# A pair's V products one step later, z's low products last, and GpSimd in program order in the first unit

## The chip, the core and the metric

One core of one Trainium2 chip. The metric is the device time of one execution in microseconds. The kernel before was timed in three runs; its profile comes from one more execution.

## What is computed

Attention with a window and a few global keys, then two feed-forward stages. The reference, cut:

```python
scores = scale * np.matmul(q, k.transpose(0, 1, 3, 2)) + bias     # q, k, v: 4 x 8 heads x 768 x 64
a = np.exp(where(keep, scores, -1e9) - max); a = a / (a.sum(-1) + 1e-9)
x = np.matmul(a, v)                                               # rows become 3072 x 512
h = x @ w_in                                                      # 512 -> 2048
z = (h * np.cos(h)) @ w_out                                       # 2048 -> 512
# then: rows with z @ w_skip > 0 go to the best of 8 experts by z @ w_gate:
y = z + gate * (np.maximum(z @ w1[e], 0) @ w2[e])                 # the other rows keep z
```

## The kernel before

The 3072 rows are worked in eight units of 384 tokens (`UT`), half a batch each. `unit(u)` runs 16 steps f, one for each block of 128 columns of w_in, and each step has two slots, 2f and 2f + 1. A step does: the h products of block f (`moe_h`, 12 matmuls of 384 columns, line 526; the weights and x are each split into a high and a low part, so three products stand for one); what is entered for the even slot; the angle, the sine and the product h cos h (`moe_g`); the split of later weight blocks (`split_hi`, `split_lo`, whose low part wi_lo is VectorE's line 492); the z products of block f - 2 (`moe_z`, line 565, nine matmuls of 512 columns into three PSUM banks, one for each tile of 128 tokens); and what is entered for the odd slot. `h cos h` is split by `split_g` into ghi (ScalarE, line 536) and glo (GpSimd, line 537). In the first unit `split_g` of a block is put off to the next step (`late_split`), behind that step's h products.

While unit u - 1 runs, the attention of unit u is worked in between, in four pairs p of heads, eight slots apart. The table `ev` (and `late`, run after `ev` and the rest of the slot) holds which part goes into which slot, counted from s0 = 32 (u - 1) + 8 p - 3: transposes of q and k (`att_Tq`, `att_Tk`) at s0 - 5 and s0 - 4; score products (`att_S`, line 396) of the three tiles at s0, s0 + 1, s0 + 2, each into two PSUM banks that VectorE empties while it adds the bias (line 401); the exponent on ScalarE, the sum's reciprocal on VectorE and the scaling of the six tiles sc on GpSimd (`att_E`, lines 415, 420, 425) late in s0 + 2; transposes of the probabilities (`att_P`, ps_p, lines 437 and 440) at s0 + 5 to s0 + 7; the products with v (`att_V`, ps_v, lines 452 and 457) at s0 + 9, which ScalarE empties into xhi (line 466) and VectorE into xlo (line 467). The rows of v before a tile are loaded into the one buffer ld_va by four DMAs on SP's queue (`att_load_va`) at s0 + 2. So the pair's values come two slots after the last ps_p, in the same slot as the second score products of the next pair, in front of them. From the second unit on, scores, transposes and values share a rotation of three PSUM banks (`ps_a`, tag "ps"). The values of the first pair go to slot 6 of a unit, of the second to slot 14, of the third to 22, of the last to 30.

The routing of a finished unit runs on VectorE in the next one: from slot 4 or 6 on, two products a slot, 27 in all (junk, line 623). Through units 1 to 6 a part of the weights is loaded again on SP's queue (ck) and checked on VectorE (cmin, line 298). In the first unit the weights are also converted, block by block (`conv_tick`: ScalarE line 212, VectorE lines 219 and 223, and in the next tick GpSimd line 230).

The order on an engine: inside `tc.manual_schedule(engines=...)` the engines named run in the order in which the program writes their work; the others are ordered by a planner that takes what it thinks is ready, the earlier in the program first. TensorE is in written order throughout, ScalarE in the units; VectorE, GpSimd and SP's queue are left to the planner in units 0 to 6. The planner's order is fixed when the program is built.

Of the kernel before, what the change touches and what calls it, by code (L numbers as in the profile page):

```python
# [20 lines left out]
P = 128  # L21
# [16 lines left out]
def kernel(  # L38
# [7 lines left out]
    NP = H // 2  # L46
# [146 lines left out]
    wo_hi = wp.tile([P, FC, DM], F32R, name="wo_hi", tag="b1")  # L193
    wo_lo = wp.tile([P, FC, DM], F32R, name="wo_lo", tag="b2")
# [81 lines left out]
    def conv_to(m, f):  # L276
        while (m, min(f, FC - 1)) not in conv_done:
            conv_tick()
# [26 lines left out]
    att = {}  # L305
# [102 lines left out]
    def att_E(u, p):  # L408
        d = att[u, p]
        sm = d["sum"]  # L410
        for t in range(HT):
            c0 = 104 if u % 2 == 0 and t == 0 else 0
            s = d["s"][t]
            for j in range(2):
                nc.scalar.activation(  # L415
                    out=s[:, j, c0:NW], in_=s[:, j, c0:NW], func=AF.Exp,
                    scale=-1.0, bias=d["m"][:, t, j:j + 1], accum_out=sm[:, t, j:j + 1],
                )
        nc.vector.tensor_scalar(out=sm, in0=sm, scalar1=1e-9, scalar2=None, op0=ALU.add)
        nc.vector.reciprocal(sm, sm)  # L420
        for t in range(HT):
            c0 = 104 if u % 2 == 0 and t == 0 else 0
            s = d["s"][t]
            for j in range(2):
                nc.gpsimd.tensor_scalar(  # L425
                    out=s[:, j, c0:NW], in0=s[:, j, c0:NW],
                    scalar1=sm[:, t, j:j + 1], scalar2=1.0, op0=ALU.mult, op1=ALU.mult,
                )
# [46 lines left out]
    zt = {}  # L475
# [82 lines left out]
    def moe_z(u, f, tiles=range(HT)):  # L558
        if f == 0 and u not in zt:
            zt[u] = [ps_z.tile([P, DM], F32, name="zp") for _ in range(HT)]  # L560
        ghi, glo = gq[u, f]
        for t in tiles:
            sl = slice(t * P, (t + 1) * P)
            for n, (a, b) in enumerate(((ghi, wo_hi), (ghi, wo_lo), (glo, wo_hi))):
                nc.tensor.matmul(  # L565
                    zt[u][t], a[:, sl], b[:, f, :],
                    start=(f == 0 and n == 0), stop=(f == FC - 1 and n == 2),
                )

# [154 lines left out]
    def at(slot, fn, *a, tail=False):  # L724
        (late if tail else ev).setdefault(slot, []).append((fn, a))
# [6 lines left out]
    for u in range(1, NU):  # L732
        for p in range(NP):
            s0 = HS * (u - 1) + PS * p - 3
            at(s0 - 12, att_load, u, p)
            at(s0 - 5, att_load_v, u, p)
            at(s0 - 5, att_Tq, u, p)
            at(s0 - 4, att_Tk, u, p)
            for t in range(HT):
                at(s0 + t, att_S, u, p, t)  # L740
                at(s0 + 5 + t, att_P, u, p, t)
            at(s0 + 9, att_V, u, p)
            at(s0 + 2, att_load_va, u, p)
            at(s0 + 2, att_E, u, p, tail=True)
    for i in range(4 * FC):
        s0 = HS + 8 + i * (HS * (NU - 2) - 24) // (4 * FC)
        at(s0, check_load, i)
        at(s0 + 2, check_min, i)
# [29 lines left out]
    for p in range(NP + 1):  # L778
        if p < NP:
            if p > 1:  # L780
                att_load_v(0, p)
            for t in range(HT):
                att_S(0, p, t)
            if p + 1 < NP:
                att_Tq(0, p + 1)
                att_Tk(0, p + 1)
            if p + 1 < NP:
                fill(p + 1)
            if p + 2 < NP:
                att_load(0, p + 2)  # L790
            att_E(0, p)
        warm(2, ps_a, "ps")
        if p > 0:
            for t in range(HT):
                att_P(0, p - 1, t)
            att_V(0, p - 1)
            if p < NP:
                att_load_va(0, p)
        conv_tick()
# [8 lines left out]
    def early():  # L808
        for s_ in range(min(list(ev) + list(late)), 0):
            run_slot(ev, s_)  # L810
            run_slot(late, s_)
        for f in range(2):
            conv_to(0, f)
            split_hi(f)
        split_lo(0)

    def unit(u):
        for f in range(FC):
            s_ = HS * u + 2 * f
            moe_h(u, f)  # L820
            if late_split:
                split_g(*late_split.pop())
            run_slot(ev, s_)
            moe_g(u, f)
            run_slot(late, s_)
            if u == 0:
                conv_to(0, f + 2)
                if f >= LAG:
                    conv_to(1, f - LAG)

            split_hi((f + 2) % FC, act=u == 0)
            split_lo((f + 1) % FC)
            if u == 0:
                for _ in range(TICKS[f % len(TICKS)]):
                    conv_tick()

                for i in range(f * E * NB0 // FC, (f + 1) * E * NB0 // FC):
                    e, j = divmod(i, NB0)
                    nc.sync.dma_start(xs[e * CAP + j * P:e * CAP + (j + 1) * P, :], pad)
            zf = u * FC + f - LAG  # L840
            if zf >= 0:
                moe_z(zf // FC, zf % FC)
                if zf % FC == FC - 1:
                    done = zf // FC
                    routes[done] = Route(rp_["p"], HT, done * UT)
                    routes[done].evac(zt[done])
            run_slot(ev, s_ + 1)
            run_slot(late, s_ + 1)
# [121 lines left out]

    with tc.manual_schedule(engines={mybir.EngineType.PE}):
        early()
        with tc.manual_schedule(engines={mybir.EngineType.Activation}):
            unit(0)
            conv_to(1, FC - 1)
        route_setup()
# [3 lines left out]
        with tc.manual_schedule(engines={mybir.EngineType.SP}):  # L980
            with tc.manual_schedule(engines={mybir.EngineType.Activation}):


                u = NU - 1
# [6 lines left out]
                for f in range(FC + 1):  # L991
# [26 lines left out]
                    if f < LAG:  # L1018
                        moe_z(u - 1, FC - LAG + f)
                        if f == LAG - 1:  # L1020
                            routes[u - 1] = Route(rp_["p"], HT, (u - 1) * UT, zpool=rp_["z"])
                            routes[u - 1].evac(zt[u - 1])
# [37 lines left out]
                with tc.manual_schedule(engines={mybir.EngineType.Pool, mybir.EngineType.DVE}):  # L1060
# [51 lines left out]
                    for n in range(NS + LAG):  # L1112
                        e, f = divmod(n, F2C)
# [13 lines left out]
                        if n >= LAG:  # L1127
                            e, f = divmod(n - LAG, F2C)
# [312 lines left out]
```

## Time and profile before

| | us |
|---|---|
| median of 3 runs | 1008.06 (1006.95 to 1009.19) |
| the profiled execution | 1010.82 |
| its span, first to last instruction | 1009.1 |
| TensorE busy in the span | 953.4 (94%) |
| VectorE busy | 751.7 (74%) |
| ScalarE busy | 535.3 (53%) |
| GpSimd busy | 532.8 (53%) |

The span runs through a first attention pass without h and z (to about 50 us), the first unit (50 to 165 us), units 1 to 6 (to about 716 us), the last unit (to about 798 us) and the experts. Busy times of TensorE include the stretches in which its clock was granted at the lower level, so a busy TensorE is not always one at its peak. In a timeline, the number in brackets is how long the engine stood before the instruction, and what let it go on.

### The profile page before, as it was taken

What the parts mean: (1) busy time and instruction counts of PE and PEld (TensorE: products, weight loads), DVE (VectorE), ACT (ScalarE), POOL (GpSimd) and SP (SyncE); (2) the same over time, 40 slices, a digit from 0 to 9 for tenths busy, and PEclk for the clock granted to TensorE, in tenths of its full rate; (3) what the DMA queues carried; (4) which work ended last, traced back from release to release, by engine and by line L of the source; (5) the groups of instructions that cost most, each with busy time, mean ns of one, the idle gap of its engine ahead of it and who ended that gap; (6) DMA issues with size and microseconds to landing.
All of it is one profiled execution on the core that took longest, in us unless ns stands there. A gap on an engine that the chain in (4) does not pass through costs nothing.

```text
span 1009.1 us, 17130 instructions
## 1 busy us (share of the span) xinstructions
PE 953.4 (94%) x5677; PEld 803.4 (80%) x5677; DVE 751.7 (74%) x1871; ACT 535.3 (53%) x1295; POOL 532.8 (53%) x707
## 2 busy tenths in 40 slices
PE   8878899999999999999999999999999889999996
PEld 4566678878878888887888788878898779999995
DVE  6679987986796689569757955885572387888882
ACT  5768878557656665665666566656463121111110
POOL 3657765545464546545454545465462355555662
PEclk7899899999999999999999999999999999999998
DMA  7497865234433443431112112100104384666400
GB/s 188 100 231 204 244 168 184 70 91 118 129 84 99 115 120 81 121 94 31 30 43 72 29 29 51 54 15 11 39 13 182 134 319 185 209 231 227 176 19 22
DMA packets 144385, 115.08 MB, mean 114 GB/s; under 512 B 100247, under 2 KB 116631, under 8 KB 144160
## 3 DMA queue, kind: packets, MB, share of 16 engines
q1 hardware_dynamic: 141056, 107.89, 36.1%
q0 software_dynamic: 3200, 5.98, 1.6%
q8 instruction: 47, 0.77, 0.3%
q14 instruction: 50, 0.41, 0.1%
q10 hardware_dynamic: 32, 0.03, 0.0%
HBM read 97.36 MB, written 21.05 MB: 117 GB/s over the span
## 4 chain that ended last, share of the span: by engine, by line
PE 57%; DVE 26%; DMA 5%; issue 5%; ACT 4%; POOL 2%; SPq 0%; POOLq 0%; ACTq 0%; DVEq 0%
PE zp L565 14%; PE hp L526 14%; DVE junk L623 9%; PE hp L946 9%; PE zp L965 9%; DVE wi_lo L492 4%; PE ps_s L396 3%; DVE r L509 2%; DVE r L552 2%; DVE sc L401 2%; DMA ck<-in_moe_w_out_dram 1%; PE ps_p L437 1%; DVE w_in_sb L223 1%; PE ps_v L457 1%; DMA st<-in_moe_w_out_dram 1%
## 5 line engine op out<-in xcount | busy, mean ns | idle before, releaser
L537 POOL TENSOR_TENSOR glo<-r,ghi 128x384 fp32r<-128x384 f32 x115 | 133.1, 1157 | 180.0 <-ACT ghi L536 149.6
L526 PE MATMUL hp<-xhi,wi_hi 128*128 128x384 f32 x492 | 177.2, 360 | 2.1 <-DVE r L552 1.3
L526 PE MATMUL hp<-xhi,wi_lo 128*128 128x384 f32 x492 | 166.9, 339 | 0.9 <-DVE wi_lo L492 0.9
L526 PE MATMUL hp<-xlo,wi_hi 128*128 128x384 f32 x492 | 165.9, 337 | 0.0
L492 DVE TENSOR_TENSOR wi_lo<-w_in_sb,wi_hi 128x512 fp32r<-128x512 f32 x128 | 114.6, 896 | 51.6 <-PE hp L526 16.8
L623 DVE CUSTOM_DVE_ANT_0 junk<-r_zr,wrep 128x512 bf16<-128x512 f32 x162 | 140.8, 869 | 8.3 <-ACT r_zr L585 6.4
L565 PE MATMUL zp<-wo_hi,ghi 128*128 128x512 f32 x345 | 146.7, 425 | 0.0
L565 PE MATMUL zp<-wo_hi,glo 128*128 128x512 f32 x345 | 137.3, 398 | 8.3 <-POOL glo L537 8.2
L565 PE MATMUL zp<-wo_lo,ghi 128*128 128x512 f32 x345 | 136.1, 395 | 0.0
L425 POOL TENSOR_SCALAR sc<-sc,sm 128x232 f32<-128x232 f32 (+1 forms) x180 | 93.6, 541 | 61.5 <-DVE sm L420 42.3
L514 ACT ACTIVATE r<-r,halfpi 128x384 f32<-128x384 f32 x128 | 79.0, 617 | 82.1 <-DVE r L509 81.0
L536 ACT CAST ghi<-r 128x384 fp32r<-128x384 f32 x115 | 59.0, 513 | 115.4 <-DVE r L552 114.3
L526 PEld LDWEIGHTS hp<-xhi,wi_hi 128*128 128x128 f32 x492 | 93.2, 189 | 16.8 <-issue 9.3
L951 ACT ACTIVATE hh<-hp 128x256 fp32r<-128x256 f32 x64 | 24.7, 387 | 152.2 <-PE hp L946 152.2
L483 POOL TENSOR_SCALAR wi_hi<-w_in_sb 128x512 fp32r<-128x512 f32 x112 | 83.7, 748 | 37.4 <-PE hp L526 32.5
L526 PEld LDWEIGHTS hp<-xhi,wi_lo 128*128 128x128 f32 x492 | 93.1, 189 | 1.2 <-DVE wi_lo L492 1.2
L526 PEld LDWEIGHTS hp<-xlo,wi_hi 128*128 128x128 f32 x492 | 93.5, 190 | 0.2
L396 PE MATMUL ps_s<-kW,qT 64*128 64x232 f32 (+1 forms) x384 | 74.0, 405 | 18.3 <-DVE xlo L467 10.8
L565 PEld LDWEIGHTS zp<-wo_hi,glo 128*128 128x128 f32 x345 | 65.6, 190 | 25.7 <-POOL glo L537 10.8
L415 ACT ACTIVATE sc<-sc,mx 128x232 f32<-128x232 f32 (+1 forms) x180 | 83.3, 464 | 3.9 <-DVE mx L401 2.7
L884 POOL TENSOR_SCALAR w2h<-we 128x512 fp32r<-128x512 f32 x64 | 46.5, 727 | 72.7 <-PE zp L965 72.7
L552 DVE TENSOR_TENSOR r<-r,hp 128x384 f32<-128x384 f32 x112 | 61.4, 549 | 25.5 <-ACT r L514 25.0
(234 smaller groups left out, 2239.6 us busy)
## 6 DMA issues: line engine op xcount, KB each, us to landing
we<-in_moe_w_dram SPq DMA_DIRECT2D x16, 2048.0 KB
st<-in_moe_w_in_dram SPq DMA_DIRECT2D x16, 512.0 KB
st<-in_moe_w_out_dram SPq DMA_DIRECT2D x16, 512.0 KB
ck<-in_moe_w_in_dram SPq DMA_DIRECT2D x32, 256.0 KB
ck<-in_moe_w_out_dram SPq DMA_DIRECT2D x32, 256.0 KB
ld_q<-in_q_dram SPq DMA_DIRECT2D x64, 96.0 KB
ld_k<-in_k_dram SPq DMA_DIRECT2D x64, 96.0 KB
ld_v<-in_v_dram SPq DMA_DIRECT2D x64, 96.0 KB
```

Source lines behind the costliest of these rows:

```text
L396: nc.tensor.matmul(sp[:, c0:NW], d["qT"][j * D:(j + 1) * D, t * P:(t + 1) * P], d["kW"][j * D:(j + 1) * D, t, c0:NW], start=True, stop=True,)
L415: nc.scalar.activation(out=s[:, j, c0:NW], in_=s[:, j, c0:NW], func=AF.Exp, scale=-1.0, bias=d["m"][:, t, j:j + 1], accum_out=sm[:, t, j:j ...
L425: nc.gpsimd.tensor_scalar(out=s[:, j, c0:NW], in0=s[:, j, c0:NW], scalar1=sm[:, t, j:j + 1], scalar2=1.0, op0=ALU.mult, op1=ALU.mult,)
L483: nc.gpsimd.tensor_scalar(out=hi, in0=ws, scalar1=1.0, scalar2=1.0, op0=ALU.mult, op1=ALU.mult)
L492: nc.vector.tensor_tensor(out=lo, in0=ws, in1=hi.bitcast(F32), op=ALU.subtract)
L526: nc.tensor.matmul(hp, a[:, c, :], b[:, c, :], start=(n == 0), stop=(n == 3 * CC - 1))
L537: nc.gpsimd.tensor_tensor(out=glo, in0=r, in1=ghi.bitcast(F32), op=ALU.subtract)
L552: nc.vector.tensor_tensor(out=r, in0=r, in1=hp, op=ALU.mult)
L565: nc.tensor.matmul(zt[u][t], a[:, sl], b[:, f, :], start=(f == 0 and n == 0), stop=(f == FC - 1 and n == 2),)
L623: nc.vector.tensor_tensor_reduce(out=junk, in0=self.zr[:, t, 0:DM], in1=self.wrep[e], op0=ALU.mult, op1=ALU.add, scale=1.0, scalar=0.0, ac ...
L946: nc.tensor.matmul(hp, a[:, c, :], b[:, c, :], start=(n == 0), stop=(n == 3 * CC - 1))
L965: nc.tensor.matmul(yq[e][j], a[:, sl], b, start=(f == 0 and n == 0), stop=(f == F2C - 1 and n == 2),)
```

## The change

Three edits. The values of a pair, where it is not the last of a unit, go two slots later, with the loads of ld_va for every pair, and the scaling of the tiles becomes a part of its own, `att_N`, entered one slot after `att_E` (the first unit's own attention, in front of the loop, calls it from `att_E` as before). `moe_z` takes the three products in the outer loop and the tiles in the inner one, so the three products with glo come last. In the first unit, and in the conversion's rest behind it, GpSimd also runs in written order.

```diff
@@ att_E
         nc.vector.reciprocal(sm, sm)
+        if u == 0:
+            att_N(u, p)
+
+    def att_N(u, p):
+        d = att[u, p]
+        sm = d["sum"]
         for t in range(HT):
@@ moe_z
         ghi, glo = gq[u, f]
-        for t in tiles:
-            sl = slice(t * P, (t + 1) * P)
-            for n, (a, b) in enumerate(((ghi, wo_hi), (ghi, wo_lo), (glo, wo_hi))):
+
+        for n, (a, b) in enumerate(((ghi, wo_hi), (ghi, wo_lo), (glo, wo_hi))):
+            for t in tiles:
                 nc.tensor.matmul(
-                    zt[u][t], a[:, sl], b[:, f, :],
+                    zt[u][t], a[:, t * P:(t + 1) * P], b[:, f, :],
@@ the table of slots
-            at(s0 + 9, att_V, u, p)
-            at(s0 + 2, att_load_va, u, p)
+            at(s0 + (9 if p == NP - 1 else 11), att_V, u, p)
+            at(s0 + 4, att_load_va, u, p)
             at(s0 + 2, att_E, u, p, tail=True)
+            at(s0 + 3, att_N, u, p)
@@ the first unit
-        with tc.manual_schedule(engines={mybir.EngineType.Activation}):
+        with tc.manual_schedule(
+            engines={mybir.EngineType.Activation, mybir.EngineType.Pool}
+        ):
             unit(0)
             conv_to(1, FC - 1)
```

## Rows read from the trace of the kernel before

**Rows 1.** Stretches: length, busy time (and instructions) of each engine, granted clock, DMA.

```profile
50.40:165.60 115.20, 98.31 (x558) 79.79 (x558) 100.41 (x190) 91.52 (x213) 75.41 (x77) 0.96 0.75 206
...
165.60:716.00 550.40, 537.45 (x3209) 450.15 (x3209) 419.12 (x1187) 343.10 (x835) 285.96 (x395) 0.99 0.27 73
...
173.60:216.70 43.10, 41.28 (x238) 34.38 (x236) 42.07 (x124) 25.03 (x62) 19.54 (x26) 0.96 0.33 93
...
207.90:211.80 3.90, 3.90 (x15) 3.76 (x15) 3.87 (x13) 3.64 (x11) 1.33 (x2) 0.58 0.25 71
...
89.50:92.30 2.80, 2.78 (x7) 2.21 (x8) 2.12 (x4) 2.39 (x7) 2.80 (x2) 0.50 0.56 162
```

**Rows 2.** TensorE's waits, 165 to 721 us: total, times, longest.

```profile
PE ps_s L396 <- DVE xlo L467: 9.8, 11, 1.5
PE ps_p L437 <- POOL sc L425: 2.7, 6, 0.5
```

**Rows 3.** TensorE's waits in the first unit.

```profile
PE zp L565 <- POOL glo L537: 8.2, 3, 3.2
```

**Rows 4.** TensorE's timeline, score 2 in first quarters: start, length, [idle before].

```profile
182.91 0.97 PE L396 MATMUL ps_s<-kW,qT 64*128 64x232 f32 x4 [0.24 <-DVE xlo L467]
...
461.21 0.97 PE L396 MATMUL ps_s<-kW,qT 64*128 64x232 f32 x4 [1.25 <-DVE xlo L467]
```

**Rows 5.** The same, second quarters, first and last of six.

```profile
207.05 0.97 PE L396 MATMUL ps_s<-kW,qT 64*128 64x232 f32 x4 [1.53 <-DVE xlo L467]
...
673.20 0.97 PE L396 MATMUL ps_s<-kW,qT 64*128 64x232 f32 x4 [1.23 <-DVE xlo L467]
```

**Rows 6.** TensorE's timeline, start of the values and of score 1.

```profile
201.33 0.44 PE L457 MATMUL ps_v<-pT,ld_v 128*64 128x128 f32 x4
...
202.58 0.66 PE L396 MATMUL ps_s<-kW,qT 64*128 64x232 f32 x4
```

**Rows 7.** VectorE's timeline in the same stretch.

```profile
205.37 0.54 DVE L509 SCALAR_TENSOR_TENSOR r<-r,hp 128x384 f32<-128x384 int32 x1
...
206.45 0.55 DVE L467 TENSOR_TENSOR xlo<-ps_v,xhi 128x384 fp32r<-128x384 f32 x1
206.92 0.38 DVE L401 CUSTOM_DVE_ANT_0 sc<-ps_s,bias_n 128x232 f32<-128x232 f32 x1
```

**Rows 8.** The chain that ended last: h products behind a wait (start, length).

```profile
208.02 3.69 PE hp L526 x12
...
302.64 2.29 PE hp L526 x12
...
579.66 3.35 PE hp L526 x12
```

**Rows 9.** Waits of SP's queue, whole span.

```profile
SPq L331 <- PE ps_v L457: 160.1, 22, 21.7
```

**Rows 10.** The chain: landing of a load of ld_va.

```profile
73.22 3.18 DMA ld_va<-in_v_dram
```

**Rows 11.** Timelines of GpSimd and TensorE, first unit.

```profile
84.16 4.18 POOL L425 TENSOR_SCALAR sc<-sc,sm 128x232 f32<-128x232 f32 x6 [1.52 <-ACT qT L356]
88.31 1.16 POOL L537 TENSOR_TENSOR glo<-r,ghi 128x384 fp32r<-128x384 f32 x1
...
89.52 0.80 PE L565 MATMUL zp<-wo_hi,glo 128*128 128x512 f32 x1 [3.24 <-POOL glo L537]
```

**Rows 12.** TensorE's timeline: z's products around a change of tile.

```profile
80.72 0.39 PE L565 MATMUL zp<-wo_hi,glo 128*128 128x512 f32 x1
80.95 0.40 PE L565 MATMUL zp<-wo_hi,ghi 128*128 128x512 f32 x1
81.19 0.39 PE L565 MATMUL zp<-wo_lo,ghi 128*128 128x512 f32 x1
```

**Rows 13.** VectorE's waits, 80 to 128 us, all of them.

```profile
DVE r L552 <- ACT r L514: 2.0, 4, 0.7
```

**Rows 14.** VectorE's timeline, its first wait for TensorE after that.

```profile
128.32 0.40 DVE L401 CUSTOM_DVE_ANT_0 sc<-ps_s,bias_n 128x232 f32<-128x232 f32 x1 [1.32 <-PE ps_s L396]
```

## The prediction

> **What bounds the kernel now.** I read the table of busy time by stretch first, then TensorE's waits, then the timelines and the chain around them. Call a unit 384 tokens; pairs of heads are 0 to 3 in a unit, and a step is one h product group with what stands beside it. In units 1 to 6 TensorE is busy 537.45 of 550.40 us, so nearly all of its time there is work; in the first unit, which also converts the weights, it is busy 98.31 of 115.20 us [rows 1]. The reader should see two different limits. In units 1 to 6 the idle time of TensorE has two names only: the score products (ps_s) waiting for VectorE's xlo, 9.8 us in 11 waits, and the transposes of the probabilities (ps_p) waiting for GpSimd's scaling sc, 2.7 us in 6 waits [rows 2]. In the first unit the biggest wait is z's third product on glo, 8.2 us in three waits [rows 3].
>
> VectorE is the second limit. From 173.60 to 216.70, the half unit in which the routing of the unit before runs on it (junk), it is busy 42.07 of 43.10 us [rows 1]. So there TensorE's waits are waits for a full engine, and a wait that is cut out returns elsewhere unless TensorE may run further ahead of VectorE than now.
>
> **Units 1 to 6: the values one step later.** Nothing is added or removed; for pairs 0 to 2 the V products, xhi, xlo and the loads ld_va move two slots (one step) later, and pair 3 stays. The score products and V share three PSUM banks in rotation. Now the order is V, score 1 (two banks), score 2: score 2 takes V's bank and waits until xlo has emptied it. After the change V stands right after the next h, with the transposes Tq behind it, and the next user of its bank after those is the first ps_p, a z and an h later. So no score product waits for xlo in pairs 0 to 2, where all 11 waits lie. I split them:
>
> - First quarter of a unit (pair 0's values): five waits, the first 0.24, the longest 1.25 us [rows 4]; they sum to 3.0. VectorE is not yet far behind there, and the score products that now follow each other find their banks empty. I take all 3.0; the bounds are 0 and 3.0.
>
> - Second quarter (pair 1's values): six waits [rows 5], the rest of the 9.8, 6.8 us. Here VectorE lags: V starts at 201.33 and score 1 at 202.58 [rows 6], so V is 1.25 us of TensorE, but VectorE reaches xlo at 206.45 and the emptying of score 1 only at 206.92, right behind it [rows 7]. After the change the second half of score 2 takes the bank of score 1's first half, so it waits for that emptying instead. If VectorE's order stays as it is with xlo cut out, that emptying starts at 206.45 and ends 0.38 later, 206.83, against 207.05 for the start now: 0.2 won, while V's 1.25 us is still owed, a loss of 1.0 per unit. If the planner of VectorE's order, which now sees score 1 follow h at once, also puts it ahead of the wrap of h and the junk that run from 205.37 to xlo [rows 7], 1.08 us, that is even; and V then fills time after the next h in which the transposes wait for the chain exponent, sum, scaling. The bounds are a loss of 1.0 and a gain of 1.53 (the longest of the waits) per unit. I take 0.4, between even and the mean wait of 1.1: 2.4 in six units.
>
> - The ps_p waits: 2.7 us [rows 2]. Score 2 to ps_p grows by V's 1.25 us of TensorE's work, and single waits are at most 0.5, so most should go. I take two thirds, 1.8; bounds 0 and 2.7.
>
> - The clock. After the waits at 207.05 and 578.69 the next twelve h products take 3.69 and 3.35 us; after the one at 301.67 they take 2.29 [rows 8]. The granted clock was 0.58 in the first of these stretches [rows 1], thus partly at 1.2 GHz after TensorE had stood. That is 1.4 and 1.06 us more, 2.5 together. Half of it goes if half the idle time goes: 1.2; bounds 0 and 2.5.
>
> att_N one slot later costs nothing: no GpSimd instruction stands between its old and its new place in these units. What hides it is GpSimd's slack; if that were gone, the ps_p waits would grow by what stands ahead. Four ld_va loads per pair move with V, past ld_v on SP's queue. SP already sits at the first of them until V is done, 160.1 us over 22 waits [rows 9]; behind it are the loads of weights for checking, which VectorE reads. The distance from V to the load stays one slot. From load to V it stays seven slots, except for pair 3, where it falls to five, 14 us at the mean slot of 550.40/192 = 2.87 us, against 3.18 us for a landing [rows 10]. Cost 0; without that cover it would be up to a landing per unit.
>
> Sum for units 1 to 6: 3.0 + 2.4 + 1.8 + 1.2 = 8.4 us.
>
> **First unit: z's order and GpSimd's order.** GpSimd scales six tiles from 84.16 and only then makes glo at 88.31; TensorE, at z's third product, stands 3.24 us until 89.52 [rows 11]. Afterwards its clock is 0.50, the 1.2 GHz level, from 89.50 to 92.30 [rows 1]. With the new program order glo of the step before comes ahead of the scalings, and z's three products with it come last, six products later; at 0.23 us a product [rows 12] that alone is 1.4 us. The waits should go from z, at the price of scalings that come one glo, 1.16 us [rows 11], later, so the first ps_p waits that much longer. In the other steps the written order (one glo, then two conversions) is nearly the one that runs now, so I cost the fixed order at 0; if an instruction stands at GpSimd's head and holds conversions back, the bound is 1.16 us in each of the three scaling steps, 3.5.
>
> The gain is not 8.2 us. From 80 to 128 VectorE idles 2.0 us in all [rows 13], and it has the conversions in its queue whatever TensorE does: an earlier z brings no earlier wrap. The first place where VectorE itself waits for TensorE is 128.32, 1.32 us [rows 14]. That is what I take: 1.3 us. Bounds: a loss of 3.5, and a gain of 8.2 plus the stretch at half clock (1.4 us of it lost, twice), 11.
>
> In the other units the z order is neutral: product starts at a change of bank (80.72 to 80.95) and inside one (80.95 to 81.19) are 0.23 and 0.24 us apart [rows 12]. The copy of z's first tile at a unit's end comes four products later, 0.9 us, seven times; ScalarE and the junk it feeds have that slack before the next z needs the banks, a step later. One rule speaks against this order. The Trainium skill ("TensorE: Matmul & The Clock Gate", section "A second HAM failure mode: psum-queue depth-cycling") tells of a kernel with 512-column products that cycles through PSUM banks and loses throughput to small gaps and a falling clock. By the rows just cited a change of bank leaves no gap here; were the rule to hold, it would be the last rival below.
>
> **Sum.** 8.4 + 1.3 = 9.7 us. The profiled execution took 1010.82 us (span 1009.1), 2.8 above the median 1008.06; 1010.82 - 9.7 = 1001.1, and against the median 998.4.
>
> **Rivals.**
> 1. VectorE stays the bound of the half unit with the junk: only half of the first quarter's waits is won, 1.5 us, the rest returns as waits for emptied score banks. 1006.6, from 1004 to 1009.5. For it: 42.07 of 43.10 us busy; against it: VectorE has idle time in the quarters after, in which it can catch up.
> 2. Slower: the second quarter loses. TensorE reaches score 2 earlier by V's time and stands until VectorE has emptied score 1; the stand grows past 2 us, and V is then paid on top: 1.0 in six units is 6.0, the clock falls in all six instead of two (4 x 1.2 = 4.9), and the scalings behind glo cost their 3.5 in the first unit; against it 3.0 + 1.8 from the rest. 6.0 + 4.9 + 3.5 - 4.8 = 9.6, so 1017.7. It decides where VectorE's order does not move score 1's emptying ahead of wrap and junk, at a lag over some 4 us after the product; the lag now is 206.92 - 202.58 = 4.3, which speaks for it. Against it: the planner orders by program place, and that place moves up.
> 3. Larger: all 12.5 us of idle time and 2.5 us of clock in units 1 to 6, and 5 us in the first unit (half of its bound): 20 us, 988. For it: VectorE's later quarters have room; against it: rivals 1 and 2's rows.
> 4. Product-outer z costs the clock: 7 x 16 groups of nine products, each 0.23 us longer at the lower level, is 232 us, 1240.
>
> **How the numbers follow.** Forecast 998.4, its own range 993 to 1004, chance 0.47. Rival 1: 0.24; rival 2: 0.15; rival 3: 0.13; rival 4: 0.01. About 0.2%, 2.0 us, is what a measurement here can tell from no change, so faster means under 1006.0 and slower over 1010.1. Faster: 0.47 + 0.13 + 0.10 of rival 1 = 0.70. Same: 0.14 of rival 1. Slower: 0.15 + 0.01 = 0.16. The range runs from 988 (half of rival 3 below it) to 1013 (most of rival 2 above), which leaves out some 0.19.
>
> **What would show it.** Right: no ps_s wait for xlo in units 1 to 6 but at most at pair 3; no z wait for glo in the first unit, which is only about 1 us shorter; ps_p waits mostly gone; h groups after score 2 at 2.3 us. Wrong: ps_s waiting for VectorE's score emptying (sc, mx) for 2 us or more in each second quarter, V or Tq waiting for banks, or VectorE's cmin waiting longer for its loads because SP sits at ld_va. If the first unit shortens by 5 us or more, my reading of VectorE as its bound fails.

## The result, and the profile after

The changed kernel took 1015.93 us (median, 1014.71 to 1018.48) against 1008.06 before: a ratio of 1.0085, 95% interval 1.0071 to 1.0098. It is slower, where 998.4 was forecast with a range up to 1013. The profiled execution's span is 1015.6 us against 1009.1.

Unit by unit (from the start of a unit's first h product to that of the next unit's; step sums further down are made in the same way from the starts of h):

| us | before | after | difference |
|---|---|---|---|
| first unit | 110.91 | 114.67 | +3.8 |
| units 1 to 6 | 555.61 | 560.03 | +4.4 |
| from unit 7 to the end | 292.2 | 290.4 | -1.8 |

So there are two losses of about the same size, in the two places where two gains were forecast.

The rows of this table, and of the tables below, come from one execution of each kernel. How far such rows agree can be read from kernels that run a stretch in the same order. In the first unit, kernels with one order on all four engines differ by up to 2.2 us (110.96 to 113.11); in units 1 to 6, kernels with one order of TensorE, VectorE and GpSimd by 1.7 us (555.20 to 556.93); and the part from unit 7 on takes 290.3 to 294.9 us where nothing in it was changed. A smaller difference shows nothing by itself.

First, TensorE's waits of the changed kernel from 165 to 725 us (total, times, longest), which answer to [rows 2]:

```profile
PE ps_s L396 <- DVE mx L401: 8.7, 9, 1.7
```

Every wait for xlo is gone and every wait of ps_p for sc, as forecast: 12.5 us of idle time in two names. In their place stands one name, the emptying of the score banks (mx). That is a third less idle time, and yet the units are longer. The granted clock is one part of it. These are stretches behind four of those stands (length; busy time and instructions of TensorE, its weight loads, VectorE, ScalarE, GpSimd; then the granted clock):

```profile
299.50:304.40 4.90, 4.90 (x15) 3.07 (x15) 4.85 (x15) 1.10 (x3) 2.44 (x2) 0.65 0.19 55
392.10:397.00 4.90, 4.90 (x15) 3.18 (x15) 4.85 (x15) 1.26 (x4) 2.22 (x2) 0.65 0.17 54
488.40:495.20 6.80, 6.80 (x20) 5.39 (x19) 6.30 (x26) 4.21 (x10) 2.80 (x4) 0.50 0.00 0
674.40:683.00 8.60, 8.60 (x26) 6.68 (x27) 8.38 (x30) 4.72 (x13) 5.46 (x7) 0.60 0.00 0
```

In all, TensorE's clock was at 1.2 GHz for 20.5 us of units 1 to 6, against 6.8 us before (one of the two stretches is in [rows 1]). Half of the difference, 6.8 us, is what the lower clock added to TensorE's own work. Not all of it reached the time: without the written order of GpSimd (an experiment below) TensorE, VectorE and GpSimd run units 1 to 6 in the same order as here, the clock is low for only 6.8 us of them, and they take 558.70 us, 1.3 less (4.5 less in steps 7 and 8, 3.1 more in the others). What such a stretch looks like on TensorE (start, length, [idle before]):

```profile
483.92 0.34 PE L532 MATMUL hp<-xhi,wi_lo 128*128 128x384 f32 x1
484.19 0.66 PE L396 MATMUL ps_s<-kW,qT 64*128 64x232 f32 x2
486.55 0.66 PE L396 MATMUL ps_s<-kW,qT 64*128 64x232 f32 x2 [1.71 <-DVE mx L401]
487.14 0.96 PE L571 MATMUL zp<-wo_hi,ghi 128*128 128x512 f32 x3
487.93 1.06 PE L571 MATMUL zp<-wo_lo,ghi 128*128 128x512 f32 x3
488.79 1.48 PE L571 MATMUL zp<-wo_hi,glo 128*128 128x512 f32 x3
```

Score 1 now follows h at once and comes in two halves. Its first head's products find a free bank, the second head's stand 1.71 us. In [rows 6] all four products ran together in 0.66 us; here each half takes 0.66 of its own. Then the clock falls, and z's three groups of three products grow from 0.96 to 1.48 us.

What the second half waits for is the bank of score 0's first half. VectorE comes to it 4.8 us after that product starts (TensorE's score 0, then VectorE):

```profile
481.31 0.66 PE L396 MATMUL ps_s<-kW,qT 64*128 64x232 f32 x4
```

```profile
482.82 1.08 DVE L498 TENSOR_TENSOR wi_lo<-w_in_sb,wi_hi 128x512 fp32r<-128x512 f32 x1
483.83 0.54 DVE L515 SCALAR_TENSOR_TENSOR r<-r,hp 128x384 f32<-128x384 int32 x1
484.29 0.68 DVE L629 CUSTOM_DVE_ANT_0 junk<-r_zr,wrep 128x512 bf16<-128x512 f32 x1
...
485.01 0.69 DVE L629 CUSTOM_DVE_ANT_0 junk<-r_zr,wrep 128x512 bf16<-128x512 f32 x1
...
485.63 0.55 DVE L558 TENSOR_TENSOR r<-r,hp 128x384 f32<-128x384 f32 x1
486.09 0.39 DVE L401 CUSTOM_DVE_ANT_0 sc<-ps_s,bias_n 128x232 f32<-128x232 f32 x1
```

Of the 8.7 us, 6.4 stand at score 1's second half in the second quarters, 1.7 at score 2 there and 0.6 in the first quarters.

In the first unit the waits changed names too (50 to 166 us; before it was z for glo, 8.2 us [rows 3], and smaller ones):

```profile
PE ps_p L443 <- POOL sc L431: 6.8, 3, 2.9
PE ps_s L396 <- DVE mx L401: 4.0, 4, 1.4
PE hp L532 <- ACT kW L371: 2.0, 1, 2.0
...
PE zp L571 <- POOL glo L543: 0.9, 1, 0.9
```

### The profile page after: what moved, and what is told of

Same layout as the page of the kernel before. It is cut to its first block, busy times and chain, and to the rows that moved or that the text cites. A ratio compares the mean times of both kernels' runs of the same rounds, so it can differ in the third digit from the quotient of the medians.

```text
span 1015.6 us, 17163 instructions
## 1 busy us (share of the span) xinstructions
PE 966.5 (95%) x5673; PEld 809.2 (80%) x5677; DVE 759.5 (75%) x1871; ACT 535.3 (53%) x1295; POOL 536.8 (53%) x707
## 5 line engine op out<-in xcount | busy, mean ns | idle before, releaser
L498 DVE TENSOR_TENSOR wi_lo<-w_in_sb,wi_hi 128x512 fp32r<-128x512 f32 x128 | 119.2, 932 | 56.0 <-PE hp L532 20.4
L629 DVE CUSTOM_DVE_ANT_0 junk<-r_zr,wrep 128x512 bf16<-128x512 f32 x162 | 138.4, 854 | 8.4 <-ACT r_zr L591 6.3
L431 POOL TENSOR_SCALAR sc<-sc,sm 128x232 f32<-128x232 f32 (+1 forms) x180 | 90.1, 521 | 67.9 <-DVE sm L420 42.4
L571 PE MATMUL zp<-wo_hi,ghi 128*128 128x512 f32 x345 | 112.2, 430 | 0.0
L532 PEld LDWEIGHTS hp<-xhi,wi_hi 128*128 128x128 f32 x492 | 93.7, 190 | 18.0 <-issue 10.2
L489 POOL TENSOR_SCALAR wi_hi<-w_in_sb 128x512 fp32r<-128x512 f32 x112 | 87.8, 784 | 36.1 <-PE hp L532 32.5
L571 PE MATMUL zp<-wo_hi,glo 128*128 128x512 f32 x345 | 102.0, 402 | 0.9 <-POOL glo L543 0.9
L571 PE MATMUL zp<-wo_lo,ghi 128*128 128x512 f32 x345 | 102.3, 403 | 0.0
L396 PE MATMUL ps_s<-kW,qT 64*128 64x232 f32 (+1 forms) x384 | 79.6, 412 | 17.3 <-DVE mx L401 14.8
L891 POOL TENSOR_SCALAR w2h<-we 128x512 fp32r<-128x512 f32 x64 | 48.6, 759 | 67.9 <-PE zp L972 67.9
L396 PEld LDWEIGHTS ps_s<-kW,qT 64*128 64x128 f32 x384 | 39.9, 195 | 54.0 <-DVE mx L401 24.4
```

Of the source, the lines that this page charges most:

```text
L396: nc.tensor.matmul(sp[:, c0:NW], d["qT"][j * D:(j + 1) * D, t * P:(t + 1) * P], d["kW"][j * D:(j + 1) * D, t, c0:NW], start=True, stop=True,)
L431: nc.gpsimd.tensor_scalar(out=s[:, j, c0:NW], in0=s[:, j, c0:NW], scalar1=sm[:, t, j:j + 1], scalar2=1.0, op0=ALU.mult, op1=ALU.mult,)
L489: nc.gpsimd.tensor_scalar(out=hi, in0=ws, scalar1=1.0, scalar2=1.0, op0=ALU.mult, op1=ALU.mult)
L498: nc.vector.tensor_tensor(out=lo, in0=ws, in1=hi.bitcast(F32), op=ALU.subtract)
L532: nc.tensor.matmul(hp, a[:, c, :], b[:, c, :], start=(n == 0), stop=(n == 3 * CC - 1))
L571: nc.tensor.matmul(zt[u][t], a[:, t * P:(t + 1) * P], b[:, f, :], start=(f == 0 and n == 0), stop=(f == FC - 1 and n == 2),)
```

## The experiments

The parts have letters below: A is the values and their va load two slots later, B the scalings one slot later as a part of their own, C z's products by kind, D GpSimd in written order in the first unit. All ratios are to the kernel before, with their 95% intervals. The lengths of units are from one profiled execution of each kernel.

### The parts alone and the whole less one

Edits: the first run has A's two lines of the change, the second C's loop, the third B and D, the fourth B, C and D.

> Only the values two slots later (and their va load two slots later); scalings, z and GpSimd as before. Theory T1 (the later values make the loss: in units 1 to 6 the wait moves from xlo to the emptying of score 1 and PE's clock falls more often, in unit 0 xhi and xlo stand behind the exponent): 1012 to 1016 us, units 1 to 6 longer by 3 to 5 us, half clock there for 15 to 25 us against 6.8 before. Theory T2 (the GpSimd order written out makes the loss, by the gaps of 2.5 to 3 us on it in unit 0): 1003 to 1008, unit 0 not longer than before's 110.9. Theory T3 (z's new order makes it): 1003 to 1008.

Measured: 1014.99 us, 1.0057 (1.0038 to 1.0077). First unit 110.96, units 1 to 6 561.09.

> Only z's products by kind, so the low part comes last. T1 and T2: 1004 to 1008; unit 0 shorter by up to 4 us, since the waits for glo go (8.2 us before) and PE then waits for other things; units 1 to 6 as before within 1 us, product spacing 241 ns as before. T3: 1012 to 1016.

Measured: 1010.63 us, 1.0010 (0.9993 to 1.0028). First unit 111.74, units 1 to 6 554.42. TensorE's waits for glo in the first unit fell from 8.2 to 5.0 us, those for mx rose from 2.2 to 4.4.

> Only the scalings one slot later as a part of their own and GpSimd in written order in unit 0; values and z as before. T1: 1006 to 1010, the waits of ps_p for sc longer by 1 to 4 us, unit 0 within 2 us of before. T2: 1011 to 1016, unit 0 longer by 4 to 7 us with gaps on GpSimd in its second half. T3: 1006 to 1010.

Measured: 1012.81 us, 1.0035 (1.0022 to 1.0047). First unit 113.72, units 1 to 6 556.72.

> All of the change but the later values: scalings one slot later, z by kind, GpSimd in written order in unit 0; values at slot 9 as before. T1: 1000 to 1006, since the saving of the glo waits in unit 0 stays (up to 7 us) and the xlo waits of units 1 to 6 stay as they were before (9.8 us in 11). T2: 1010 to 1015, unit 0 as long as in the changed kernel (114.7). T3: 1010 to 1015 with units 1 to 6 longer.

Measured: 1016.34 us, 1.0072 (1.0053 to 1.0091). First unit 115.42, units 1 to 6 555.26.

No single theory survives. A alone costs 5.5 us in units 1 to 6 and nothing in the first unit, and without A units 1 to 6 are as before. B, C and D together cost 4.5 us in the first unit and nothing in units 1 to 6. The fourth run's time, 1016.34, lay above every range given for it, and the second's, 1010.63, between its ranges. The parts don't add up: A alone costs 0.57%, B, C and D together 0.72%, and the whole 0.85%. Taking A off the whole leaves the median where it was (1016.34 against 1015.93): units 1 to 6 are 4.8 us shorter in the profile, but the first unit is 0.8 and the part from unit 7 on 2.9 us longer, both no more than such stretches differ by between executions. My expectation that in the first run the clock would carry the loss was wrong: its clock was low for only 3.4 us of units 1 to 6. The stretches behind its stands at 297.51 (1.24 us) and 486.63 (1.70 us), which are stands as the changed kernel has them, read 1.00 where the changed kernel's read 0.65 and 0.50:

```profile
486.70:493.50 6.80, 6.16 (x27) 4.49 (x27) 6.68 (x20) 2.91 (x5) 3.61 (x3) 1.00 0.00 0
297.60:302.20 4.60, 3.96 (x15) 2.41 (x15) 4.55 (x14) 1.10 (x3) 2.45 (x2) 1.00 0.18 59
```

So the clock is a loss that may or may not come on top; there must be another. The sums of the 16 steps over units 1 to 6 show where. V stood in steps 3, 7, 11 and 15 and moves to 4, 8 and 12. The columns: v_late is A alone; v_p0 and v_p1 are A for the first pair alone and for the second alone, the next experiments:

| us, six units | before | v_late | after | v_p0 | v_p1 |
|---|---|---|---|---|---|
| steps 3 + 4 | 77.10 | 77.29 | 75.75 | 75.22 | 77.38 |
| steps 5 + 6 | 67.69 | 61.94 | 61.43 | 61.43 | 67.74 |
| step 7 | 51.98 | 52.49 | 54.37 | 61.02 | 44.06 |
| step 8 | 32.18 | 39.63 | 41.28 | 34.96 | 38.07 |
| steps 11 + 12 | 71.81 | 72.71 | 72.42 | 71.84 | 71.84 |

In steps 11 and 12, where no wait stands, 8.2 us leave step 11 and 9.1 come to step 12 in v_late: the move as such costs 0.6 to 0.9 us. In steps 5 and 6 there is a gain of 6 us. In step 7 the same 8 us of products leave, and the step doesn't get shorter.

### Which pair's values, and which half of B and D

Edits: A for the first pair alone, and for the second pair alone (the lines are those for the first); then B alone, D alone.

```
-            at(s0 + 9, att_V, u, p)
-            at(s0 + 2, att_load_va, u, p)
+            at(s0 + (11 if p == 0 else 9), att_V, u, p)
+            at(s0 + (4 if p == 0 else 2), att_load_va, u, p)
```

> Values (and their va load) two slots later for each unit's first pair alone; pairs 1 to 3 as before; nothing else changed. Theory U (in the seventh step of a unit VectorE sets the time, and the second pair's values there were work done inside its lag; the first pair's values, moved, cover the scalings that its neighbour waits for): moving the first pair's saves the 4.4 and 1.3 us that steps 5 and 6 of units 1 to 6 lost in the run with all values later, and costs about 1 us in steps 2 to 4: units 1 to 6 together 549 to 552 us (555.6 before), time 1003 to 1006. Rival W (later values cost in each place, since the two scores ahead of them then follow each other too closely): units 1 to 6 556 to 558, time 1008 to 1011.

Measured: 1013.04 us, 1.0032 (1.0019 to 1.0045). First unit 110.06, units 1 to 6 559.36.

> Values (and their va load) two slots later for each unit's second pair alone; nothing else changed. Theory U: step 7 of units 1 to 6 stays within 1 us of its 52.0 us although 8 us of TensorE's work have left it, and step 8 grows by 7 to 9 us: time 1014 to 1018. Rival W: a quarter to a third of the loss of the run with all values later, step 7 shorter by 6 to 8 us: 1009 to 1012.

Measured: 1010.79 us, 1.0015 (1.0000 to 1.0031). First unit 113.32, units 1 to 6 554.70.

Both results are the reverse of what theory U asked for in time. Rival W's numbers hold for the second run and are passed by the first, which does save in steps 5 and 6 what U asked (6.3 us). The second pair's values, moved alone, let step 7 go by their whole 7.9 us. The first pair's, moved alone, save 8.2 us up to step 6, and step 7 grows by 9.0. TensorE's waits from 166 to 721 us, first pair's values moved, then second pair's:

```profile
PE ps_s L396 <- DVE xlo L467: 11.5, 6, 2.4
PE ps_s L396 <- DVE mx L401: 3.1, 5, 0.8
```

```profile
PE ps_s L396 <- DVE mx L401: 3.7, 6, 1.0
PE ps_s L396 <- DVE xlo L467: 3.3, 5, 1.5
PE ps_p L437 <- POOL sc L425: 2.7, 6, 0.5
PE zp L565 <- POOL glo L537: 0.5, 1, 0.5
```

The first fence is the point. The second pair's values stand where they stood, VectorE's work is the same, and the six waits for xlo in the second quarters have grown from 6.8 to 11.5 us: TensorE arrives earlier at a VectorE that doesn't. Over the six, VectorE starts to empty score 0 there 24.8 us after the products in sum, against 19.8 before. Behind those stands the clock falls in four units instead of two. With the second pair's values away instead, xlo and one gate product no longer stand ahead of score 1's emptying: from the start of score 0's emptying to that of score 1's VectorE takes 22.2 us in the six quarters, against 30.2 before. That difference, 8.0 us, is what step 7 gives up. The theory left after this, U2: VectorE's pace sets the time from step 3 to 8, and what TensorE gains ahead of it TensorE waits for.

> Only the scalings one slot later as a part of their own; GpSimd ordered by the planner as before, values and z as before. If the later scalings are what lengthens unit 0 by 2.8 us in the run with both: 1011 to 1013, ps_p waiting for sc 4 to 5 us in unit 0. If the written GpSimd order is: 1007 to 1010, and ps_p's waits as before (1.4 us).

Measured: 1009.43 us, 0.9998 (0.9985 to 1.0011). First unit 112.27.

> Only GpSimd in written order in unit 0, the scalings written where they were, right after the exponent; values and z as before. If the written order is what lengthens unit 0: 1011 to 1014, z waiting for glo as long as before or longer, since the scalings stand ahead of glo and wait for the sums. If the later scalings are: 1006 to 1010.

Measured: 1013.20 us, 1.0041 (1.0020 to 1.0062). First unit 116.88 in the profiled execution, whose span, 1017.0, is above that median.

B alone costs nothing, and GpSimd's order in units 1 to 6 stays what it was; D alone costs time, and B and D together (1012.81) more than B alone.

### The whole less D, and VectorE's gate products issued later

Edits: the change without its last hunk; and, for the spread,

```
-            first, step, *then = (6, 0.55, 23, 25, 26, 27) if u == 0 else (4, 0.5, 21, 23, 24, 25)
+            first, step, *then = (6, 0.7, 25, 27, 28, 29) if u == 0 else (4, 0.75, 24, 26, 27, 28)
```

> The whole change but GpSimd's written order in unit 0: later values, scalings a slot later, z by kind, GpSimd ordered by the planner. Theory D (the written order alone costs unit 0 its 3 to 4 us, as the run with that order alone was 1.0041 of before and the one with the scalings alone 0.9998): unit 0 110 to 113 us (114.7 with the whole change), units 1 to 6 as with the whole change, 558 to 561: time 1011 to 1014. Rival E (unit 0 is set by VectorE, and any saved wait for glo turns up as a wait for VectorE and as time at half clock, whatever GpSimd's order): unit 0 114 to 116, time 1014 to 1017.

Measured: 1012.96 us, 1.0040 (1.0024 to 1.0057). First unit 109.66 (a little under theory D's 110), units 1 to 6 558.70: theory D, and against rival E. Some of GpSimd's own waits from 50 to 165 us, in the whole change and then without D:

```profile
POOL sc L431 <- PE hp L532: 9.9, 1, 9.9
POOL glo L543 <- ACT ghi L542: 9.5, 4, 4.3
...
POOL sc L431 <- DVE sm L420: 1.7, 3, 1.0
```

```profile
POOL sc L431 <- DVE sm L420: 7.7, 4, 2.4
...
POOL glo L543 <- ACT ghi L542: 1.1, 2, 0.6
```

In written order glo sits at GpSimd's head and waits up to 4.3 us for ScalarE's ghi, with the weight conversions behind it; in the planner's order it waits 1.1 us in all, and the scalings wait instead. (The stand of 9.9 us ends at 52.96, and most of it lies ahead of the unit.) One conversion that GpSimd starts 29.4 us into the unit without D starts at 38.4 with it. Over the first unit GpSimd is idle for 41.2 us with the written order (busy 73.51 of 114.67) and for 37.1 without (72.52 of 109.66). That D costs the time is shown, by the three pairs of kernels that differ in it alone (3 to 4 us in the medians); that it does so by these waits of glo alone is only the likeliest reading.

> The kernel before, with VectorE's 27 gate products of a unit issued over 20 slots instead of 13 (and the steps of the routing behind them 3 slots later), so that VectorE has slack in steps 4 to 8 of units 1 to 6, where it is busy 42 of 43 us. Theory U2 (in units 1 to 6 VectorE's lag sets the time up to step 8, so what TensorE gains ahead of that it waits for there): the waits for xlo at step 7 (6 to 7 us over the units, with 3.4 us of half clock) mostly go: units 1 to 6 548 to 552 us, time 1001 to 1006. Rival W (later values cost by themselves): says nothing of this run but that the waits may stay; 1006 to 1010.

Measured: 1008.73 us, 0.9998 (0.9983 to 1.0013). Units 1 to 6 553.43.

> The same spread of VectorE's gate products, with the values two slots later and nothing else of the change. Theory U2: the gain of 4 to 8 us that the later values bring up to step 6 is no longer given back at step 7: 3 to 7 us under the run with the spread alone, 996 to 1001. Rival W: still 4 to 7 us over the run with the spread alone, 1006 to 1012.

Measured: 1016.49 us, 1.0067 (1.0042 to 1.0092). Units 1 to 6 558.71.

These two decide nothing: VectorE isn't in written order, and the planner put the products where they had been. The 27 of the first routed unit start over 39.0 us in both the kernel before (172.6 to 211.6) and the spread (175.3 to 214.3).

### Half the gate products, and VectorE in written order

Edits: `logits_v` over the first half of the columns; VectorE added to the engines in written order for units 1 to 6, with the spread above and the loads of the weights' test kept to the second half of a unit.

```
-                out=junk, in0=self.zr[:, t, 0:DM], in1=self.wrep[e], op0=ALU.mult, op1=ALU.add,
+                out=junk[:, 0:DM // 2], in0=self.zr[:, t, 0:DM // 2],
+                in1=self.wrep[e][:, 0:DM // 2], op0=ALU.mult, op1=ALU.add,
```

> The kernel before with VectorE's gate products over the first 256 of 512 columns (the other half of each product is left out, so the routing is by other numbers): some 9 us of VectorE's 43 in steps 3 to 8 of each of units 1 to 6 gone. Theory U2 (VectorE's lag sets the time up to step 8): step 7 of units 1 to 6 falls from 52.0 to 43 to 46 us over the six, step 5 and 6 stay; units 1 to 6 545 to 549 us, time 997 to 1003. Rival W (the second quarter is not set by VectorE): step 7 above 49, time 1005 to 1010.

Measured: units 1 to 6 545.97 us, step 7 46.58. The whole kernel took 1088.64 us, since other rows go to other experts behind the units; only units 1 to 6 are compared.

> The same half of the gate products, with the values two slots later. Theory U2: now step 7 gives up the 8 us of TensorE's work that have left it (34 to 38 us), and what the later values save at steps 5 and 6 (4 to 6 us) is kept: 2 to 6 us under the run with half the products alone. Rival W (later values cost by themselves): 4 to 7 us over it, as without the halving.

Measured: units 1 to 6 547.49 us (whole 1093.71), step 7 42.82, step 8 38.07.

The first is as U2 said, step 7 just above its range: 9.6 us come out of units 1 to 6 when VectorE has less to do there. The waits from 166 to 721 us without and with later values:

```profile
PE ps_s L396 <- DVE xlo L467: 2.2, 2, 1.9
PE ps_p L437 <- POOL sc L425: 1.4, 6, 0.3
PE ps_s L396 <- DVE mx L401: 0.8, 3, 0.4
PE zp L565 <- POOL glo L537: 0.4, 1, 0.4
```

```profile
PE ps_s L396 <- DVE mx L401: 4.9, 5, 1.4
```

The second is half right. Later values cost 1.5 us now instead of 5.5, so about 4 of the 5.5 are VectorE's lag; 1.5 is within what two executions of one order differ by. Steps 5 and 6 keep 5.1 us of gain, as U2 asked. But no gain is left over: steps 3 and 4 lose 2.8, steps 7 and 8 lose 3.7 (step 7 falls to 42.8, not to 34 to 38) and steps 11 and 12 lose 1.1. The waits for xlo that later values would remove were down to 2.2 us already, and score 1's second half waits for mx in the first two of these units (1.3 and 1.4 us).

> The kernel before with VectorE in written order in units 1 to 6, its 27 gate products issued over 20 slots instead of 13 and the loads and minima of the weights' test kept to the second half of each unit. Nothing left out. Theory U2: the lag of VectorE up to step 8 shrinks by 5 to 7 us of its work, and with it the stand at step 7: 1001 to 1007, if the written order makes no new wait of its own; if it does, up to 1030, with VectorE standing at the head of its queue for ScalarE or TensorE. Rival W: 1007 or more, whichever order.

Measured: 1121.02 us, 1.1137 (1.1094 to 1.1180).

> The same written order of VectorE, with the values two slots later. Theory U2: 2 to 6 us under the run with the written order alone. Rival W: 4 to 7 us over it.

Measured: 1090.45 us, 1.0817 (1.0789 to 1.0844).

Both say nothing on U2, since another wait covers all: the low part of w_in stands behind whatever VectorE's written order has at its head (166 to 800 us, the first of the two):

```profile
PE hp L526 <- DVE wi_lo L492: 80.6, 46, 3.4
```

### Taking work off VectorE, then off GpSimd

Edits: w_in's low part on GpSimd in steps 3 to 7 of units 1 to 6; and, in the last run, its high part on ScalarE in steps 2 to 8.

```
-            split_lo((f + 1) % FC)
+            split_lo((f + 1) % FC, eng=nc.gpsimd if u > 0 and 3 <= f <= 7 else nc.vector)
```

```
-            split_hi((f + 2) % FC, act=u == 0)
+            split_hi((f + 2) % FC, act=u == 0 or 2 <= f <= 8)
```

> The kernel before with the low part of w_in made on GpSimd instead of VectorE at steps 3 to 7 of units 1 to 6 (0.7 us each on VectorE, so about 3.6 us of its 43 in steps 3 to 8; GpSimd is busy 20 of 43 us there). Nothing left out. Theory U2 (VectorE's lag sets the time up to step 8): step 7 of units 1 to 6 falls from 52.0 to 46 to 50 us over the six, units 1 to 6 549 to 553 us (555.6 before, 546.0 with half the gate products), time 1002 to 1007. Against it: wi_lo on GpSimd comes later and the products of the first layer wait for it; then time 1010 or more, with PE waiting for wi_lo.

Measured: 1028.48 us, 1.0189 (1.0162 to 1.0216). Units 1 to 6 572.78, step 7 50.23. TensorE didn't wait for wi_lo, as was named against it, but for GpSimd's sc (7.3 us) and glo (5.4) and for the score banks.

> The same, with the values two slots later. Theory U2, as the runs with half the gate products left it: units 1 to 6 1 to 5 us over the run without later values (5.5 with all of VectorE's work, 1.5 with half the gate products), time 1004 to 1011. If the later values had a gain of their own that VectorE's lag takes back: 2 to 5 us under it.

Measured: 1035.19 us, 1.0256 (1.0232 to 1.0280). Units 1 to 6 580.84, 8.1 us over the run before it, more than U2's 1 to 5; the clock was low for 30.7 us of them, against 10.2.

> The kernel before with the high part of w_in made on ScalarE instead of GpSimd at steps 2 to 8 of units 1 to 6 (0.60 us each there, 0.62 on GpSimd). Nothing left out; VectorE's own work is the same. If GpSimd's instructions stretch VectorE's: the gate products' mean falls from 869 ns to 800 to 840, step 7 of units 1 to 6 from 52.0 to 45 to 50 us, units 1 to 6 548 to 554 us (555.6 before), time 1001 to 1007. If only the amount of VectorE's work counts: mean and step 7 as before, 1007 to 1011. Against both: ScalarE, in written order, gets to the rounding and the sine of its neighbours later by up to 0.6 us a step: z or the first layer's products wait for it, 1010 to 1016.

Measured: 1014.93 us, 1.0053 (1.0034 to 1.0072). Units 1 to 6 561.26, step 7 44.80, in an execution of 1018.70 us, above that median.

Here is VectorE's work from 166 to 717 us (count; busy time, mean ns of one; idle time before): the kernel before, the low part on GpSimd, the high part on ScalarE.

```profile
L623 DVE CUSTOM_DVE_ANT_0 junk<-r_zr,wrep 128x512 bf16<-128x512 f32 x162 | 140.8, 869 | 8.3 <-ACT r_zr L585 6.4
...
L552 DVE TENSOR_TENSOR r<-r,hp 128x384 f32<-128x384 f32 x95 | 52.1, 548 | 19.8 <-ACT r L514 19.5
```

```profile
L623 DVE CUSTOM_DVE_ANT_0 junk<-r_zr,wrep 128x512 bf16<-128x512 f32 x162 | 160.5, 991 | 8.9 <-ACT r_zr L585 6.4
...
L552 DVE TENSOR_TENSOR r<-r,hp 128x384 f32<-128x384 f32 x92 | 50.5, 549 | 19.3 <-ACT r L514 18.9
```

```profile
L623 DVE CUSTOM_DVE_ANT_0 junk<-r_zr,wrep 128x512 bf16<-128x512 f32 x162 | 123.9, 765 | 8.3 <-ACT r_zr L585 6.3
```

VectorE's gate products get longer when GpSimd gets work and shorter when GpSimd loses it, with their number and size unchanged. Giving 30 operations of 0.7 us to GpSimd cost VectorE 19.7 us on the gate products alone, nearly what it had saved, and GpSimd took 1.72 us for each. In the last run step 7 falls by 7.2 us, as U2 asks when VectorE's lag shrinks; but steps 5 and 6 are 12.4 us longer, which gives VectorE time to catch up as well, so this run doesn't tell the two apart. The time is worse, for the reason named against it: h now waits for the weights.

```profile
PE hp L526 <- DVE wi_lo L492: 8.6, 10, 1.4
PE ps_p L437 <- POOL sc L425: 3.5, 6, 1.0
PE hp L526 <- ACT wi_hi L481: 2.7, 5, 1.0
```

Steps 2, 5, 6 and 10 lose 1.7, 4.1, 8.3 and 3.5 us. No version here beats the kernel before by what can be measured; B alone, C alone and the spread alone are equal to it.

## Why the prediction was wrong, point by point

**What bounds it.** Right in the reading: VectorE, 42 of 43 us busy, sets the half unit with the gate products. The prediction wrote that a wait cut out there returns elsewhere, and then summed as though it did not.

**First quarter and ps_p, +3.0 and +1.8.** The waits went, and the gain was larger than the 4.8 said: 1.3 us in steps 3 and 4 (net of the move itself, which was costed at nothing and takes 0.6 to 0.9 in steps 11 and 12), and 6.3 in steps 5 and 6, where 1.8 was taken from 2.7 us of waits. A row of waits counts only the gaps; the ps_p products also ran closer together (9.5 us beside their gaps in these steps before, 7.2 after).

**Second quarter, +2.4. This is the step that failed.** Steps 7 and 8 lost 11.5 us. The prediction priced one stand, score 2 behind the emptying of score 1. It had no term for score 1, whose second half takes the bank of score 0's first half once V no longer stands between them: there TensorE stood 6.4 us in these quarters, because VectorE came to score 0's emptying 3.1 to 4.8 us after the product's start (2.9 to 3.8 before). And the term was added to the first quarter's gain. The two are gains over the same VectorE, and v_p0 shows the first handed over whole at step 7. V's own products come on top: they left step 7 without shortening it, and in step 8 they cost 7 to 9 us. Alone, the second pair's move is worth -7.9 + 5.9, a gain of 2.0 near the 2.4 of the term; but 3.4 of it is clock not lost that time, which the sum counted elsewhere, so the agreement is luck.

This is close to rival 2 (1017.7 said, 1015.93 measured), with its "V is then paid on top" and its mark, ps_s waiting for mx in the second quarters, though at 0.5 to 1.7 us, not past 2. Its condition held but in part: VectorE's order moved score 1's emptying ahead of one gate product, not of the wrap of h, and it begins 4.9 to 6.1 us after the first half's products, against 3.0 to 4.3 before. What the rival shares with the prediction is that it looks for the stand at score 2.

**Clock, +1.2.** It went the other way: 20.5 us at 1.2 GHz against 6.8, in one execution; what of that reached the time is said above. Like stands left 3.4 us of low clock in v_late, 13.7 in v_p0, and 6.8 in the whole change without D, whose order in these units is the same. Half the idle time doesn't mean half of the low clock. What decides whether a stand brings the clock down was not found.

**First unit, +1.3.** z's waits for glo went from 8.2 to 0.9 us and bought nothing, as forecast in kind; VectorE gave no earlier work. The fixed order, costed at 0 with a bound of 3.5, is where the step failed: with D the first unit takes 114.67, without it 109.66, more than the bound, and D alone makes the kernel 1.0041 of before. Without D the unit is 1.3 us shorter than before, the number forecast, but no more than two executions of one order differ by. The mechanism named for the bound, an instruction at GpSimd's head holding conversions back, fits the waits and the conversion that starts 9 us late. The error was to call the written order "nearly the one that runs now" from one step of the trace. Why C on top of B and D costs the kernel 3.5 us (1016.34 against 1012.81) was not followed to its end; in the first unit, 1.7 us longer, the clock was low for 23.9 us against 6.8 us without C.

**z's order.** Neutral alone, as said: 1.0010 with 1 inside its interval, product starts 231 ns apart (median, units 1 to 6) in both kernels, and the clock low for 3.4 us of units 1 to 6 against 6.8 before. Rival 4 is out.

**The loads of va.** The loads and their place on SP's queue show in no wait of TensorE in units 1 to 6.

## What to carry to other kernels

Two gains that are both measured against the same full engine are one gain at most; before summing, ask for each stretch which engine's own pace ends it, and count products that leave such a stretch as paid in full where they go. When an order of products changes, ask of each of them, not only of the one that waits now, whose bank it takes next and when that bank is emptied. A written order for a queue has to be judged by what stands at its head in every step, since one instruction that waits holds back work that the planner would have let through. And an instruction issued later in the program is not later on an engine whose order a planner makes.

## What the runs showed of the hardware

A part of GpSimd's work is paid for by VectorE. In the kernel before, two gate products in a row (start, length), and what GpSimd did beside them:

```profile
202.33 0.68 DVE L623 CUSTOM_DVE_ANT_0 junk<-r_zr,wrep 128x512 bf16<-128x512 f32 x1
...
203.05 1.38 DVE L623 CUSTOM_DVE_ANT_0 junk<-r_zr,wrep 128x512 bf16<-128x512 f32 x1
```

```profile
202.67 1.21 POOL L537 TENSOR_TENSOR glo<-r,ghi 128x384 fp32r<-128x384 f32 x1 [3.11 <-PE ps_v L457]
203.85 1.06 POOL L483 TENSOR_SCALAR wi_hi<-w_in_sb 128x512 fp32r<-128x512 f32 x1
```

The one that starts ahead of glo takes 0.68 us, the one that starts inside it 1.38, and it ends 0.55 after glo does. Over units 1 to 6, 72 of the 162 products start while no GpSimd instruction runs, and take 652 to 695 ns; the 90 that start inside one take 1018 ns on average. Against 0.68 each, that is 30 of their 140.8 us. With the low part on GpSimd 114 start inside one, with the high part on ScalarE 43. VectorE's operations with one operand in PSUM (r with hp, 548 and 549 ns in the rows of the last experiment) don't change. The Trainium skill ("SBUF — State Buffer", section "SBUF: two separate sides") says that a VectorE operation with two inputs in SBUF and a GpSimd operation that reads SBUF share one pair of ports under an exclusive lock, and that whichever comes second waits; these rows agree.

Two score products of 64 rows, one for each head, run at the same time: four instructions in 0.66 us in [rows 6]. When the second head's bank is still full they run one after the other, 0.66 us each, so a split score takes about 0.66 us more beside its wait, and 0.35 more than a score 2 behind its wait for xlo (0.97 in [rows 4]). No row of waits counts that. In units 1 to 6, scores took 55.1 us from the end of the product before them in the kernel before and 63.8 in v_late, 2.7 of the 8.7 us in gaps.
